# An attention-plus-MLP kernel: MLP units of one chunk and four feature blocks, paired score bursts, two uncast loads, and a new order of all work

## The chip, the cores and the metric

One core of one Trainium2 chip. The metric is the device time of one execution in microseconds (us), lower is better. A profile of one execution goes with each kernel; its span is about 1.8 us shorter than the time of the same execution. In the profiles PE is TensorE, PEld its weight loads, DVE VectorE, ACT ScalarE and POOL GpSimd. A run is called slow in the record when it is over 1.5% above the fastest of the same kernel, else fast. The clock is the share of its full rate that TensorE was granted; at half rate its matmuls start twice as far apart.

## The reference

Four batches, eight heads, 768 tokens, head size 64: causal attention with a decay per head and a running state, then an MLP with ELU on 3072 tokens of width 512.

```python
for b in range(nb):                                   # along the sequence
    intra = (qb @ kb.T * Dmask) @ vb                   # inside the block
    inter = (qb * lam_pow) @ kv_state                  # from the blocks before
    out[:, :, sl] = intra + inter
    kv_state = lam_block * kv_state + (kb * rev_pow).T @ vb
x = attn_out.transpose(0, 2, 1, 3).reshape(3072, 512)
h = x @ w_in                                           # 512 x 2048
g = where(h > 0, h, exp(min(h, 0)) - 1)
return g @ w_out                                       # 2048 x 512
```

## The kernel before

The work is cut into 24 chunks of 128 tokens (chunk g is batch g mod 4, step g div 4). For each chunk TensorE transposes q and k (later chunks: by DMA), computes the scores S, multiplies them with v and with the state (P), and updates the state (U). The MLP takes three chunks at a time, one block of 128 features per slot. In the profiles psT, psS, psO and psU hold the results of transposes, scores, attention output and state update, psH and psM those of the MLP's first and second product; wi and wo are its weights, g is the ELU's output. The code is shortened, its comments are mine:

```python
TC = 3; MT = TC * L                       # 3 chunks, 384 columns
WI = [2, 2, 4, 4, 4]; WO = [4, 4, 4, 4]   # blocks per weight transfer
M2_FIRST = 12                             # first slot with a second product
POOL_ORDER = "i0 i1 l3 k0 i2 k1 i3 k2 i4 l4 k3 o0 k4 k5 o1 l6 o2 k6 k7 o3 l8 l10"

def mm1(s):                               # one feature block of 3 chunks
    m, n = divmod(s, NFT)
    pH = ps.tile([128, MT], FP32, tag=tag, ...)
    for kk in range(NHP):                 # 4 matmuls of 384 columns
        nc.tensor.matmul(pH[:], lhsT=wi16[i][:, kk, j*128:(j+1)*128],
                         rhs=xt[m][:, kk, :], start=(kk == 0), stop=(kk == NHP - 1))
    e = msb.tile([128, MT], FP32, tag="e", bufs=3, ...)
    nc.scalar.activation(e[:], pH[:], AF.Exp)
    nc.scalar.activation(pH[:], pH[:], AF.Relu)
    return e, pH
...
def regular(g, f):                        # attention of chunk g from slot f
    at(f, lambda: att_S(g))               # 8 matmuls on 64 rows, then 2 masks
    at(f + 2, lambda: att_PI(g, (0, 1)))
    at(f + 2, lambda: att_PI(g, (2, 3)))
    at(f + 3, lambda: att_X(g))
    at(f + 3, lambda: att_U(g))
...
emit_load(0, "q")                         # GpSimd (software) queue, cast fp32 -> fp16
emit_load(0, "k")
...
att_T_pe(0, ...); att_S(0); att_T_pe(1, ...); att_S(1); open_PV_X(0, ...)
att_T_pe(2, ...); att_S(2); open_PV_X(1, ...); open_PV_X(2, ...)
# only then the first mm1
```

## Time and profile before

| | before |
|---|---|
| time, median of the runs beside the result | 231.94 us (231.19 to 233.45) |
| span of the profiled execution (timed 233.71) | 231.9 us |
| first score, first unit of product 1, first of product 2 | 7.61, 17.09, 39.73 us |
| full stretch, one chunk | 24.94 us for three = 8.31 us |
| from the last matmul's end (227.9) to the end | 4.0 us |

This is TensorE's timeline of the kernel before, with start, length, line, operation and count:

```profile
39.73 1.46 PE L364 MATMUL psM<-wo,g 128*128 128x512 f16 x3
40.99 1.49 PE L339 MATMUL psH<-xt,wi 128*128 128x384 f16 x4
42.27 0.92 PE L364 MATMUL psM<-wo,g 128*128 128x512 f16 x3
43.02 0.81 PE L339 MATMUL psH<-xt,wi 128*128 128x384 f16 x4
```

Starts are 1.26 and 1.28 us apart where 0.65 is the full pace. After the 2.15 us wait that ends at 39.19 the array runs at half rate for about 3 us.

### The profile page before, as it was taken

The numbers are of one execution on the slowest core, as the hardware profiler recorded it, in microseconds if no ns is written. First come the engines' busy times: TensorE is split into PE (matmuls) and PEld (weight loads), VectorE is DVE, ScalarE is ACT, GpSimd is POOL, SyncE is SP. The second block draws the span as 40 slices with busy tenths as digits, with TensorE's granted clock in tenths as the row PEclk, the third lists the DMA queues.
The fourth block names the chain that finished last, engine by engine and source line by source line (L and its number), as shares of the span: only waits on it lengthen the run. The fifth ranks groups of instructions, "written<-read, shape, count | busy, mean of one in ns | idle before, by whom it ended". The sixth has DMA issues, their size and how long they took to land.

```text
span 231.9 us, 4127 instructions
## 1 busy us (share of the span) xinstructions
PE 208.7 (90%) x1504; PEld 117.7 (51%) x1504; DVE 144.7 (62%) x274; ACT 134.0 (58%) x306; POOL 87.5 (38%) x101
## 2 busy tenths in 40 slices
PE   1488666989999999999999999999999999999993
PEld 0364443546546555555654555555555555555441
DVE  6665867476686676766667667676765657344410
ACT  4437765366575565755566555755576557667610
POOL 8999274797773274445256242200000000000000
PEclk9999998899999999999999999999999999999998
DMA  7999999999999998997977990540033001100312
GB/s 50 137 160 195 177 149 164 156 148 156 156 132 211 165 132 34 184 156 117 93 47 189 147 74 3 173 98 3 1 115 68 3 0 71 69 0 0 136 48 90
DMA packets 100324, 24.39 MB, mean 105 GB/s; under 512 B 92496, under 2 KB 97360, under 8 KB 100304
## 3 DMA queue, kind: packets, MB, share of 16 engines
q0 software_dynamic: 79152, 13.63, 81.6%
q1 hardware_dynamic: 21152, 10.50, 21.9%
q8 instruction: 12, 0.20, 0.4%
q14 instruction: 8, 0.07, 0.1%
HBM read 27.27 MB, written 6.29 MB: 145 GB/s over the span
## 4 chain that ended last, share of the span: by engine, by line
PE 76%; POOL 8%; DVE 6%; DMA 4%; ACT 3%; issue 2%; POOLq 0%; ACTq 0%; DVEq 0%
PE psM L364 34%; PE psH L339 31%; DMA kn<-in_k_dram 4%; PE psO L278 4%; PE psS L257 3%; POOL qn L93 2%; PE psO L283 2%; POOL wi L118 2%; POOL kn L93 2%; POOL vz L97 2%; DVE st L321 1%; POOL kd L205 1%; PE psU L305 1%; DVE g L350 1%; DVE qT L230 1%
## 5 line engine op out<-in xcount | busy, mean ns | idle before, releaser
L339 PE MATMUL psH<-xt,wi 128*128 128x384 f16 x512 | 104.5, 329 | 3.3 <-DVE g L350 1.4
L350 DVE SCALAR_TENSOR_TENSOR g<-e,psH 128x384 f16<-128x384 f32 x128 | 70.4, 552 | 58.9 <-ACT psH L345 58.1
L344 ACT ACTIVATE e<-psH 128x384 f32<-128x384 f32 x128 | 63.0, 492 | 72.5 <-PE psH L339 72.0
L364 PE MATMUL psM<-wo,g 128*128 128x512 f16 x384 | 101.6, 382 | 0.0
L339 PEld LDWEIGHTS <-wi 128*128 128x128 f16 x512 | 50.0, 99 | 49.3 <-issue 6.3
L345 ACT ACTIVATE psH<-psH 128x384 f32<-128x384 f32 x128 | 62.4, 487 | 0.0
L364 PEld LDWEIGHTS <-g 128*128 128x128 f16 x384 | 34.8, 98 | 29.5 <-issue 1.0
L263 DVE TENSOR_TENSOR pp<-psS,mask 128x512 f16<-128x512 f32 x48 | 30.9, 686 | 5.7 <-PE psS L257 4.0
L205 POOL TENSOR_TENSOR kd<-kn,ks 128x512 f16<-128x512 f16 x20 | 20.9, 1048 | 11.2 <-DMA kn<-in_k_dram 10.3
L317 POOL TENSOR_TENSOR stt<-st,upp 64x256 f32<-64x256 f16 x24 | 14.6, 607 | 27.3 <-DVE st L321 26.4
L97 POOL DMA_DIRECT2D vz<-in_v_dram x14 | 15.3, 1095 | 21.0 <-PE psU L305 17.6
L257 PE MATMUL psS<-qT,kT 64*128 64x128 f16 x192 | 10.4, 232 | 7.6 <-DVE st L321 2.1
L278 PE MATMUL psO<-pp,vz 128*128 128x128 f16 x168 | 16.2, 219 | 0.0
L93 POOL DMA_DIRECT2D qn<-in_q_dram x14 | 15.8, 1128 | 0.8 <-POOLq L509 0.8
L93 POOL DMA_DIRECT2D kn<-in_k_dram x14 | 15.2, 1089 | 1.0 <-DMA qn<-in_q_dram 1.0
L321 DVE TENSOR_TENSOR st<-stt,psU 64x256 f16<-64x256 f32 x32 | 13.3, 417 | 3.3 <-PE psU L305 1.0
L278 PEld LDWEIGHTS <-vz 128*128 128x128 f16 x168 | 13.6, 98 | 2.6
L283 PE MATMUL psO<-qT,st 128*128 128x128 f16 x80 | 14.4, 219 | 0.0
L257 PEld LDWEIGHTS <-kT 64*128 64x128 f16 x192 | 6.1, 99 | 15.0 <-issue 6.1
L379 ACT COPY osb<-psM 128x512 f32<-128x512 f32 (+1 forms) x16 | 8.5, 576 | 8.7 <-PE psM L364 8.7
L377 DVE COPY osb<-psM 128x512 f32<-128x512 f32 (+1 forms) x9 | 5.9, 656 | 8.4 <-PE psM L364 5.7
L296 DVE TENSOR_TENSOR xt<-psO,qs 128x512 f16<-128x512 f32 x16 | 10.9, 683 | 0.0
(48 smaller groups left out, 83.7 us busy)
## 6 DMA issues: line engine op xcount, KB each, us to landing
out_dram<-osb SPq DMA_DIRECT2D x23, 256.0 KB, 2.3
qn<-in_q_dram POOLq DMA_DIRECT2D x10, 256.0 KB, 9.1
kn<-in_k_dram POOLq DMA_DIRECT2D x10, 256.0 KB, 9.8
vz<-in_v_dram POOLq DMA_DIRECT2D x10, 256.0 KB, 9.5
wo<-in_moe_w_out_dram POOLq DMA_DIRECT2D x4, 512.0 KB, 9.0
wi<-in_moe_w_in_dram POOLq DMA_DIRECT2D x3, 512.0 KB, 7.9
qn<-in_q_dram POOLq DMA_DIRECT2D x4, 128.0 KB, 4.1
kn<-in_k_dram POOLq DMA_DIRECT2D x4, 128.0 KB, 4.3
```

Source lines behind the costliest of these rows:

```text
L93: nc.gpsimd.dma_start(out=t[:].rearrange("p b h d -> p (b h) d"), in_=src(x))
L97: nc.gpsimd.dma_start(out=t[:, :, 0::2, :].rearrange("p b h d -> p (b h) d"), in_=src(v))
L205: nc.gpsimd.tensor_tensor(out=kd[:], in0=of(kg, g), in1=ks[:].unsqueeze(2).broadcast_to([128, H, 64]), op=ALU.mult,)
L257: nc.tensor.matmul(pts[hh][:, hp, :], lhsT=kt[r, hp, :], rhs=qt[r, hp, :], start=True, stop=True,)
L263: nc.vector.tensor_tensor(out=P[:], in0=pts[hh][:], in1=mask[:, hh::2, :], op=ALU.mult)
L278: nc.tensor.matmul(po[:, hp, :], lhsT=vt[:, b0 : b0 + 2, :], rhs=Pt[(g, hh)][:, hp, :], start=(hh == 0), stop=(hh == 1 and cb == 0), skip_ ...
L283: nc.tensor.matmul(po[:, hp, :], lhsT=st[b][cb % 2][:, hp, :], rhs=qt[:, hp, :], start=False, stop=True, skip_group_check=True,)
L339: nc.tensor.matmul(pH[:], lhsT=wi16[i][:, kk, j * 128 : (j + 1) * 128], rhs=xt[m][:, kk, :], start=(kk == 0), stop=(kk == NHP - 1),)
L344: nc.scalar.activation(e[:], pH[:], AF.Exp)
L345: nc.scalar.activation(pH[:], pH[:], AF.Relu)
L350: nc.vector.scalar_tensor_tensor(out=g[:], in0=e[:], scalar=-1.0, in1=r[:], op0=ALU.add, op1=ALU.min)
L364: nc.tensor.matmul(psM[m][c][:], lhsT=gts[s][:, c * 128 : (c + 1) * 128], rhs=wo16[i][:, j, :], start=(n == 0), stop=(n == NFT - 1),)
```

## The change

The intent: begin the MLP as soon as one chunk is ready, give TensorE in each moment something whose data has come, and switch less often to the 64-row matmuls of the scores. Both weight matrices come in pieces of two blocks, the two interleaved. The whole order is a written list: `1:g:j` is product 1 of chunk g and blocks 4j to 4j+3, `2:g:j` product 2; T, S, E, P, U are transposes, scores, their masks, output and state update; V, Z, v, z zero buffers. The core of the diff, shortened, with comments of mine:

```diff
-    TC = 3
-    M2_FIRST = 12
-    WI = [2, 2, 4, 4, 4]
-    WO = [4, 4, 4, 4]
-    POOL_ORDER = "i0 i1 l3 k0 i2 k1 i3 k2 i4 l4 k3 o0 ... l10"
+    FB = 4
+    GPE = 10                     # transposes on TensorE for 10 chunks, was 8
+    WI = [2] * 8
+    WO = [2] * 8
+    POOL_ORDER = ("iota q1 k1 v1 v0 i1 i0 k2 q2 v2 o0 o1 i3 i2 q3 i5 k3 o2 d0 o3 ... v10")
+    RAW = "q0 k0"                # uncast, on the hardware queue
+    FIRST = "q0:0 c0 k0:1 c1 c2"
+    OPEN = (
+        "V0 Z1 z1 V1 z0 v3:1 Z0 z3 z2 T0 T1 S0 S1 P0 P1 1:0:0 T2 1:1:0 S2 2:0:0 Z2 P2 1:2:0 "
+        "1:0:1 2:1:0 1:1:1 U0 T3 2:2:0 1:2:1 S3 2:0:1 2:1:1 1:0:2 1:1:2 P3 2:2:1 ... S8:9 2:6:0 E9")
...
-            nc.tensor.matmul(
-                pH[:], lhsT=wi16[i][:, kk, j * 128 : (j + 1) * 128],
-                rhs=xt[m][:, kk, :], start=(kk == 0), stop=(kk == NHP - 1),
-            )
+        for f in range(FB):
+            i, w = wi_of[j * FB + f]
+            for kk in range(NHP):
+                nc.tensor.matmul(
+                    pH[:, f, :], lhsT=wi16[i][:, kk, w * 128 : (w + 1) * 128],
+                    rhs=xt[g][:, kk, :], start=(kk == 0), stop=(kk == NHP - 1),
+                )
...
+            else:                # "S4:5": both score bursts, then the mask of the first
+                att_S(a[0])
+                att_S(a[1])
+                att_E(a[0])
...
+    prog[-1] += ":1"             # the last product 2 is computed in two column halves
```

## The prediction

> **What bounds the kernel now.** I read the page's busy rows first, then the groups, then TensorE's timeline in the opening, in the middle and at the end.
>
> ```profile
> span 231.9 us, 4127 instructions
> PE 208.7 (90%) x1504; PEld 117.7 (51%) x1504; DVE 144.7 (62%) x274; ACT 134.0 (58%) x306; POOL 87.5 (38%) x101
> PE   1488666989999999999999999999999999999993
> PEclk9999998899999999999999999999999999999998
> GB/s 50 137 160 195 177 149 164 156 148 156 156 132 211 165 132 34 184 156 117 93 47 189 147 74 3 173 98 3 1 115 68 3 0 71 69 0 0 136 48 90
> L339 PE MATMUL psH<-xt,wi 128*128 128x384 f16 x512 | 104.5, 329 | 3.3 <-DVE g L350 1.4
> L364 PE MATMUL psM<-wo,g 128*128 128x512 f16 x384 | 101.6, 382 | 0.0
> L263 DVE TENSOR_TENSOR pp<-psS,mask 128x512 f16<-128x512 f32 x48 | 30.9, 686 | 5.7 <-PE psS L257 4.0
> ```
>
> TensorE is full from about slice 9 (5.8 us each) to the end and half empty before; nothing else is over 62%. The means of 329 and 382 ns are latencies; the pace has to be read from starts. TensorE's timeline, in the opening and in the full stretch:
>
> ```profile
> 17.09 3.48 PE L339 MATMUL psH<-xt,wi 128*128 128x384 f16 x16
> 22.06 0.82 PE L339 MATMUL psH<-xt,wi 128*128 128x384 f16 x4 [1.05 <-DMA wi<-in_moe_w_in_dram]
> 30.50 0.40 PE L223 MATMUL psT<-ident,kn 128*128 128x128 f16 x4 [1.28 <-DMA kn<-in_k_dram]
> 39.19 0.61 PE L257 MATMUL psS<-qT,kT 64*128 64x128 f16 x8 [2.15 <-DVE st L321]
> ...
> 115.25 0.81 PE L364 MATMUL psM<-wo,g 128*128 128x512 f16 x3
> 115.90 0.81 PE L339 MATMUL psH<-xt,wi 128*128 128x384 f16 x4
> 116.64 0.40 PE L257 MATMUL psS<-qT,kT 64*128 64x128 f16 x8
> 116.97 0.82 PE L364 MATMUL psM<-wo,g 128*128 128x512 f16 x3
> 117.63 0.81 PE L339 MATMUL psH<-xt,wi 128*128 128x384 f16 x4
> ```
>
> Start to start, four 384-column matmuls take 0.65 us (162.5 ns each), three of 512 columns 0.65 us (215.5 ns), and eight score matmuls 0.33 us plus about 0.10 us lost around them (the preceding four start 0.74 before instead of 0.65). Elsewhere in that timeline twelve 128-column matmuls, each with its own weight load, run from 43.67 to 44.34: 56 ns each.
>
> At those paces TensorE's work is 512 x 0.1625 = 83.2 (first MLP product), 384 x 0.2155 = 82.8 (second), attention output 272 x 0.056 = 15.2, state updates 80 x 0.056 = 4.5, transposes of 8 chunks 64 x 0.056 = 3.6, scores 24 x 0.43 = 10.3: 199.6 us. The span is 32.3 more. Up to 17.09 only 3.9 us of that work (24 transposes, 3 scores, 24 output products) is done: 13.2 lost. From 17.09 to 40 the counts (52 of the 384-column kind, 20 updates, 20 outputs, 24 transposes, 3 scores) make 13.3 of 22.9: 9.6 lost. The tail after the last matmul (227.9) is 4.0. That leaves 5.5 for everything from 40 to 218, most of it before 70. So the gain to be had lies in the first 40 us, where the MLP waits until three chunks have gone through attention, and then for weights, keys and states.
>
> **What the Trainium skill says.** "TensorE: Matmul & The Clock Gate", section "Wait — 56ns, not 53.3ns?", gives N ÷ 2.4 GHz + about 2.5 ns start to start: 55.6 ns at 128 columns, 215.7 at 512. The trace agrees (56; 162.5 at 384; 215.5). Hence cutting 384 columns into 3 x 128 costs about 3 x 56 - 162.5 = 5.5 ns per old matmul. The same page, "What's actually happening", says that an idle array falls to half rate. The trace agrees: at 8.15 four transposes take 0.54 us, and in slices 7 and 8, after the idle ends at 39.19, the clock row shows 8. "DMA: Bandwidth & Descriptors", section "Issuing engines are not separate DMA queues", says that all issuers share 16 engines and that a second issuer saves only issue time. So the two loads moved to the hardware queue free about 1.9 us of GpSimd issue (1.06 + 0.88 in the trace), not bandwidth. "VectorE: DVE Perf Modes", section "The TRN2 errata — SBUF-src ops pay a fixed extra latency per instruction", says what each operation pays besides its elements; here VectorE's ELU takes 552 ns at 384 columns, and the score product 686 at 512, so I estimate 690 for the new 512-column ELU.
>
> **The change part by part.**
>
> *MLP units.* A unit is now 16 matmuls of 128 columns (0.90 us) or 4 of 512 (0.86). 1536 x 0.056 = 86.0, so +2.8 us. ELU, Exp and Relu go from 128 to 96 each: VectorE 96 x 0.69 = 66 instead of 70; ScalarE's pair at about 0.62 each (copies of 512 columns take 0.59) 119 instead of 125. Per chunk of 8.3 us of TensorE, ScalarE has about 5.6 and VectorE 5.6: no new bound in the steady part.
>
> *Scores in pairs.* 24 bursts become 14 (four single, ten double): 24 x 0.33 + 14 x 0.10 = 9.3, so -1.0 us. Transposes by TensorE for ten chunks instead of eight: 80 x 0.056 = 4.5, +0.9. New sum of TensorE's work: 202.3, that is +2.7.
>
> *The opening.* The arrival of data is the ruler. In slices 2 to 8 the transfers move 163 GB/s on average, and with the first load landed at 4.8 us this puts the old fourth key pair (4.19 MB of half-precision data in the order of issue) at 4.8 + 4.06/0.163 = 29.7; TensorE waited for it until 30.5. In the new order, counting the uncast k as 0.2 MB: weights i0, i1 at 12.5, o1 at 18, i2 at 21, k3 24.5, o3 28, i7 38, k4 43. VectorE and ScalarE reach the first scores at about 9.7 (five zeroings of 0.4 to 0.6 us stand on ScalarE before the first kT copy; in the old kernel scores start at 7.6), the first output is copied by 13.4, and the first MLP unit starts at 13.5 instead of 17.09. It goes on with whatever chunk is ready, and the second product no longer waits until 39.7 but starts when o1 lands, near 18-19. From 21 on the listed order has nearly always something whose data has come; each pair of units waits for an ELU about 2.1 us after the end of the unit two before. Walking the order with these durations I get to 47 at the end of unit 1:3:2 (first product, chunk 3, third group of four blocks; 2:... is the second product). Up to there TensorE does 16 x 0.90 + 12 x 0.86 + 6 x 0.45 (transposes) + 4 x 0.43 + 4 x 0.45 + 2 x 0.22 = 31.3 us, so 15.7 are lost. The old kernel loses 13.2 + 9.6 + about 2 = 24.8 by then. Gain: 9 us.
>
> *48 to 75 us.* Four transposed chunks, five pairs of score products, six updates of which four take four VectorE operations, and eleven ELUs: VectorE has about 25.7 us of work beside 29 of TensorE. That is tight, and I put 3 us of waiting on it (the old kernel loses about 3.5 after 47 in all).
>
> *Rest.* 1 us of small ELU waits in the steady part. Tail: the last output goes out in two halves, so one 0.37 us copy and then the store, 3.1 us in the trace: 3.5 instead of 4.0.
>
> Sum: 202.3 + 15.7 + 3.0 + 1.0 + 3.5 = 225.5. The timed median of before is within 0.4 of its profiled span, so I take the span for the time.
>
> **The rivals.**
>
> *Weight loads bind.* 128-column matmuls need a load every 56 ns, 16 in a row and up to 30 with neighbours; the trace shows only runs of 12 at that pace. Were a pair to take 64 ns, 1536 x 8 ns = 12 us would eat the gain: about 237. Against it: those 12 run at full pace, and a 0.86 us unit of four loads follows nearly every burst, so the queue can refill. I give it 5%.
>
> *The opening stays as long.* If the many short rows of q, k, v or the uncast loads slow the transfers to the 137 of slice 2, k4 lands at 49 and the gain shrinks to 4 us: about 230. For it: the new order asks for all weights before q4, k4; the old one had k4 at 30.5. Against it: chunks 0 to 3 alone hold 28 us of MLP work, which covers that.
>
> *VectorE in the middle.* With 25.7 of 29 us taken, each score product ahead of an ELU holds up the two psH buffers; if that costs 6 us instead of 3: 228.5.
>
> *Better than I walk.* TensorE unbroken from 21 us on, with the waits in the middle filled by the order: 220.
>
> **Range and chances.** The gain of the opening (9, give or take 4) against 2.7 of added work decides it; the error of the walk is about 4 us either way, hence 220.5 to 230. The 2% line is 227.6, 2.1 above the middle, so faster 0.68, within 2% 0.30; slower needs the weight-load rival or a deadlock of orders: 0.02.
>
> **What would show it.** Right: first psH matmul near 13.5 us; first psM near 18-19; 16 psH matmuls in about 0.90 us start to start; one chunk per 8.3 us in the steady part; transposes of chunk 4 near 45; ScalarE and VectorE under 70%; a tail of 3.5. Wrong: psH units of 1.0 us or more with issue as the reason; psH waiting for g throughout; chunk 4's keys after 48; first scores far from 9.7; a clock row under 9 after 25 us.

## The result, and the profile after

The changed kernel takes 223.12 us (222.66 to 223.24, 4 runs) against 231.94 beside it: ratio 0.9608, 95% interval 0.9556 to 0.966. Ratios here are the mean time of one kernel's fast runs over that of the other's of the same rounds, so not quite the ratio of the medians quoted. The point forecast was 225.5, the range 220.5 to 230.

Rows of the page of the changed kernel (busy times; busy tenths, clock and transfer rate in 40 slices of 5.5 us; groups):

```profile
span 221.4 us, 6086 instructions
PE 207.1 (94%) x2548; PEld 156.3 (71%) x2548; DVE 138.6 (63%) x238; ACT 134.8 (61%) x255; POOL 88.6 (40%) x102
PE   0598999999999999999999999999999999999993
PEclk9999999999999999999999999999999999999999
GB/s 114 169 182 186 195 200 167 139 169 120 166 140 181 127 164 135 141 84 93 143 100 100 132 108 95 144 0 98 94 3 98 96 3 47 52 1 50 47 3 95
L388 PE MATMUL psH<-xt,wi 128*128 128x128 f16 x1536 | 102.2, 220 | 1.8 <-ACT xt L333 0.7
L409 PE MATMUL psM<-wo,g 128*128 128x512 f16 (+1 forms) x388 | 97.6, 377 | 0.8 <-DVE osb L422 0.5
```

TensorE is at 80% or more from the third slice instead of about the eighth, its clock row never falls under 9, and the first slice moves 114 GB/s instead of 50. Neither row tells the whole opening: the first unit's 16 matmuls take 1.71 us (13.36 to 15.07 below), half the later pace, though slice 3 shows a 9 for the clock.

TensorE's timeline of the changed kernel, opening, full stretch and end:

```profile
9.48 1.09 PE L300 MATMUL psS<-qT,kT 64*128 64x128 f16 x16 [1.26 <-ACT kT L289]
...
13.36 1.91 PE L388 MATMUL psH<-xt,wi 128*128 128x128 f16 x16
15.07 0.63 PE L281 MATMUL psT<-ident,qn 128*128 128x128 f16 x4
...
17.43 1.04 PE L409 MATMUL psM<-wo,g 128*128 128x512 f16 x4
...
28.71 1.95 PE L388 MATMUL psH<-xt,wi 128*128 128x128 f16 x32
30.50 0.61 PE L322 MATMUL psO<-pp,vz 128*128 128x128 f16 x8
...
45.00 1.06 PE L388 MATMUL psH<-xt,wi 128*128 128x128 f16 x16
45.99 0.62 PE L300 MATMUL psS<-qT,kT 64*128 64x128 f16 x16
...
85.86 1.07 PE L388 MATMUL psH<-xt,wi 128*128 128x128 f16 x16 [0.45 <-DVE g L376]
86.86 0.62 PE L300 MATMUL psS<-qT,kT 64*128 64x128 f16 x16
87.41 1.04 PE L409 MATMUL psM<-wo,g 128*128 128x512 f16 x4
88.29 1.06 PE L388 MATMUL psH<-xt,wi 128*128 128x128 f16 x16
...
217.73 0.60 PE L409 MATMUL psM<-wo,g 128*128 128x256 f16 x4 [0.52 <-DVE osb L422]
```

The 32 matmuls from 28.71 to 30.50 take 56 ns each with a weight load apiece: the weight loads do not bind in such a run. The score bursts repeat every 16.50 us (86.86, 103.36, 119.86), so a chunk costs 8.25 us. By stretches (length; busy time and count of TensorE, weight loads, VectorE, ScalarE, GpSimd; clock; transfers), the changed kernel does not wait from 100 to 133 us, and it idles 0.23 us in the stretch in which VectorE is nearly full:

```profile
50.00:60.00 10.00, 9.77 (x135) 8.03 (x134) 9.45 (x17) 7.10 (x14) 10.00 (x10) 1.00 1.56 141
100.00:133.00 33.00, 33.00 (x418) 25.04 (x417) 21.51 (x36) 19.45 (x37) 15.76 (x18) 1.00 1.10 113
```

Where the 10.5 us between the two profiled spans come from, at the paces of the traces (a lone score burst at 0.445 us, a pair at 0.67; see a1_single_scores for these): TensorE's work goes from 199.9 to 201.4, the tail from 4.0 to 3.6 (3.1 after the last matmul and the 0.52 us wait), and what is left, waiting and half rate, from 28.0 to 16.4. The gain is 11.6 us less of these. The profiled execution of before was one of its slower ones (233.71 timed), which is the reason that this difference is larger than the 8.8 us of the medians.

### The profile page after: what moved, and what is told of

It is laid out like the page before. It is cut to its first block, busy times and chain, and to the rows that moved or that the text cites. A ratio compares the mean times of both kernels' runs of the same rounds, so it can differ in the third digit from the quotient of the medians.

```text
span 221.4 us, 6086 instructions
## 1 busy us (share of the span) xinstructions
PE 207.1 (94%) x2548; PEld 156.3 (71%) x2548; DVE 138.6 (63%) x238; ACT 134.8 (61%) x255; POOL 88.6 (40%) x102
## 4 chain that ended last, share of the span: by engine, by line
PE 79%; DVE 11%; ACT 5%; DMA 2%; issue 1%; SPq 0%; DVEq 0%; ACTq 0%
PE psH L388 34%; PE psM L409 33%; PE psO L322 5%; DVE g L376 3%; PE psS L300 3%; DVE stt L356 2%; DMA raw_k<-in_k_dram 2%; PE psO L327 2%; DVE pp L309 2%; PE psU L344 2%; DVE qT L288 1%; DVE st L360 1%; ACT e L393 1%; ACT psH L394 1%; PE psT L281 1%
## 5 line engine op out<-in xcount | busy, mean ns | idle before, releaser
L388 PEld LDWEIGHTS <-wi 128*128 128x128 f16 x1536 | 94.0, 98 | 22.0 <-issue 2.2
L388 PE MATMUL psH<-xt,wi 128*128 128x128 f16 x1536 | 102.2, 220 | 1.8 <-ACT xt L333 0.7
L393 ACT ACTIVATE e<-psH 128x512 f32<-128x512 f32 x96 | 57.3, 597 | 68.3 <-PE psH L388 68.0
L409 PE MATMUL psM<-wo,g 128*128 128x512 f16 (+1 forms) x388 | 97.6, 377 | 0.8 <-DVE osb L422 0.5
L376 DVE SCALAR_TENSOR_TENSOR g<-e,psH 128x512 f16<-128x512 f32 x96 | 65.6, 684 | 44.1 <-ACT psH L394 42.8
L394 ACT ACTIVATE psH<-psH 128x512 f32<-128x512 f32 x96 | 56.9, 593 | 0.0
L335 DVE TENSOR_TENSOR xt<-psO,qs 128x512 f16<-128x512 f32 x14 | 9.7, 691 | 11.9 <-PE psO L327 11.9
L424 ACT COPY osb<-psM 128x512 f32<-128x512 f32 (+1 forms) x24 | 13.9, 579 | 4.5 <-PE psM L409 4.5
L288 DVE TENSOR_TENSOR qT<-psT,qs 128x512 f16<-128x512 f16 x10 | 6.6, 681 | 5.2 <-PE psT L281 5.2
L281 PE MATMUL psT<-ident,qn 128*128 128x128 f16 x40 | 4.6, 247 | 5.4 <-DVE qn L122 5.4
L333 ACT CAST xt<-psO 128x512 f16<-128x512 f32 x10 | 5.9, 588 | 6.0 <-PE psO L322 4.0
```

Of the source, the lines that this page charges most:

```text
L376: nc.vector.scalar_tensor_tensor(out=g[:], in0=e[:], scalar=-1.0, in1=r[:], op0=ALU.add, op1=ALU.min)
L388: nc.tensor.matmul(pH[:, f, :], lhsT=wi16[i][:, kk, w * 128 : (w + 1) * 128], rhs=xt[g][:, kk, :], start=(kk == 0), stop=(kk == NHP - 1),)
L409: nc.tensor.matmul(psM[g][:, cols], lhsT=gts[(g, j)][:, f, :], rhs=wo16[i][:, w, cols], start=first and f == 0, stop=end and f == FB - 1, ...
```

## The experiments

Names with a start from the changed kernel, with b from the kernel before. Each ran with five timed rounds and a profile. They came in three groups, each on one chip with its own runs of the kernel before (medians 233.65, 234.19 and 233.39, with a scatter from 231.5 to 237.2). Since the changed kernel scatters by under 1 us and the kernel before by several, I compare the a-kernels by their own times and spans and quote the ratios only beside them. The changed kernel itself ran beside the result and in the third group only, so the differences quoted for a1 to a6 cross groups; "over the first measurement" is meant where nothing else is said. All results were correct.

| run | time, us (range) | ratio to before | profiled span |
|---|---|---|---|
| a0_again (unchanged) | 222.56 (222.43 to 223.37) | 0.957 | 220.7 |
| a1_single_scores | 225.65 (225.06 to 226.21) | 0.967 | 224.0 |
| a2_soft_q0k0 | 224.22 (223.79 to 224.62) | 0.961 | 222.0 |
| a3_three_first | 226.57 (226.24 to 228.46) | 0.973 | 225.0 |
| a4_wi_first | 234.98 (234.45 to 235.4) | 1.007 | 232.7 |
| a5_zeros_late | 222.11 (221.96 to 223.04) | 0.953 | 220.4 |
| a6_tail_banks | 222.39 (221.61 to 222.96) | 0.953 | 220.4 |
| a7_both | 221.64 (221.43 to 222.67) | 0.952 | 220.8 |
| a8_three_undone | 231.38 (230.41 to 231.84) | 0.993 | 229.8 |
| b1_split128 | 233.29 (232.86 to 233.8) | 1.000 | 232.0 |
| b2_raw_q0k0 | 230.20 (230.12 to 230.69) | 0.987 | 228.4 |
| b3_kept_warm | 232.35 (231.33 to 232.85) | 0.997 | 230.4 |

**a0_again.** The changed kernel itself, no edit, in the third group.

> The changed kernel itself, as the yardstick on this chip for the three that run beside it: 223 to 224.5 us, profiled span near 221.4.

222.56 us, half a microsecond under the first measurement. Spans of 220.7 to 221.6 over its six executions. So differences of about half a microsecond between groups are not read below.

**a1_single_scores.** Scores in bursts of one chunk.

```diff
-            (f"S{g}:{g + 1}", AT["S"]), (f"E{g + 1}", AT["S"] + 1),
+            (f"S{g}", AT["S"]), (f"S{g + 1}", AT["S"] + 1),
```

(and likewise S4, S6, S8 in the opening list.)

> The changed kernel with the scores of each chunk in a burst of its own, one unit apart (24 bursts instead of 14). My theory: each burst costs about 0.11 us of exposed weight load beside its 0.33, so +1.1 us over the changed kernel: about 224.2, ratio to before near 0.966. Rival, that the pairing is a main source of the gain: 226 or more. Rival, that the pairing is worth nothing because TensorE waits elsewhere anyway: 223.1.

225.65 us, 2.5 over the first measurement of the changed kernel and 2.6 in span: more than twice the 1.1 expected. TensorE's timeline of this run:

```profile
89.17 1.06 PE L388 MATMUL psH<-xt,wi 128*128 128x128 f16 x16
90.16 0.40 PE L300 MATMUL psS<-qT,kT 64*128 64x128 f16 x8
90.49 1.04 PE L409 MATMUL psM<-wo,g 128*128 128x512 f16 x4
91.37 1.06 PE L388 MATMUL psH<-xt,wi 128*128 128x128 f16 x16
```

Eight scores stand for 0.33 us (90.16 to 90.49), sixteen in the changed kernel for 0.55 (86.86 to 87.41). So eight cost 0.22 and each burst a fixed 0.11 on top; with the 0.10 before it and 0.02 after it, a burst costs about 0.22 beside its work. Ten fewer bursts are 2.2 us (the scores of chunks 0 and 1 stand together in both kernels, 16 at 9.48); the period of two chunks confirms it (16.71 us here, from 87.97 to 104.68, against 16.50). I had taken the 0.33 as pure work. The runs show the size of this cost and not its cause.

**a2_soft_q0k0.** The two loads back on the software queue.

```diff
-    RAW = "q0 k0"
-    FIRST = "q0:0 c0 k0:1 c1 c2"
-        "iota q1 k1 v1 v0 ...
+    RAW = ""
+    FIRST = "c0 c1 c2"
+        "iota q0 k0 q1 k1 v1 v0 ...
```

> The changed kernel with q, k of chunk 0 cast by the software queue again, first in its order; no cast instructions. My theory: the hardware queue saves only about 1.9 us of GpSimd issue for all that follows, and the first scores wait for zeroings on ScalarE in any case: 223.1 to 224.6 (the first MLP unit at 13.4 to 14.5 us). Rival, that the two uncast loads carry the early start: 226 or more, first MLP unit after 15.5 us.

224.22 us, +1.1 (span +0.6). The first unit starts at 13.82 instead of 13.36. The second unit still runs at half pace (1.85 us to the next start, 16.35 to 18.20, instead of 1.19), and the scores of chunk 4 start at 47.09 instead of 45.99. As expected, and the rival falls; but the ratio (0.961) is that of the change itself, so the 1.1 us rest on comparing groups and on the trace.

**a3_three_first.** No MLP unit before the third chunk.

```diff
-        ... P0 P1 1:0:0 T2 1:1:0 S2 2:0:0 Z2 P2 1:2:0 "
+        ... P0 P1 T2 S2 Z2 P2 1:0:0 1:1:0 2:0:0 1:2:0 "
```

> The changed kernel with the old rule of starting: no MLP unit before the third chunk has gone through attention (two first-product units and one second-product unit move behind the output of chunk 2, nothing else moves). My theory, that the early start fills TensorE's idle time: +2 to +3 us, 225 to 226. Rival, that data arrival sets the end of the opening and the early units are hidden anyway: 223.1 to 223.6.

226.57 us, +3.4 (span +3.6), somewhat over the expected 2 to 3: the first unit starts at 17.98, the first of product 2 at 21.79, and no later slack takes the delay up (chunk 4's scores start at 49.16 instead of 45.99). The rival, that arrival of data hides the early units, falls. Not all of it is waiting:

```profile
17.98 3.62 PE L388 MATMUL psH<-xt,wi 128*128 128x128 f16 x32
21.79 1.64 PE L409 MATMUL psM<-wo,g 128*128 128x512 f16 x4 [0.19 <-DVE g L376]
23.27 1.95 PE L388 MATMUL psH<-xt,wi 128*128 128x128 f16 x32
```

The 32 matmuls take about 3.5 us instead of 1.8, the four of 512 columns 1.48 instead of 0.86: 2.3 us over full pace, where the changed kernel's first two units lose 1.0. So I estimate that about 1.3 of the 3.4 us are half pace.

**a4_wi_first.** All of the first weight matrix before the second.

```diff
-        ... q2 v2 o0 o1 i3 i2 q3 i5 k3 o2 d0 o3 i4 v3 o5 o4 d2 o7 i6 d3 d1 i7 o6 q4
+        ... q2 v2 i3 i2 q3 i5 k3 i4 d0 i6 i7 v3 o0 o1 d2 o2 o3 d3 d1 o5 o4 o7 o6 q4
```

> The changed kernel with all eight pieces of the first weight matrix issued before any of the second, as the kernel before has it; TensorE's order is not touched. My theory, that the interleaved arrival of the two matrices is what lets both products start early: TensorE stands at the first second-product unit (17.4 us in the changed kernel) until the piece lands near 24, 4 to 7 us lost: 227 to 230. Rival, that arrival is not binding: under 224.

234.98 us: 11.9 slower, as slow as the kernel before (ratio 1.007), and more than the 4 to 7 expected. TensorE's timeline:

```profile
27.23 1.01 PE L409 MATMUL psM<-wo,g 128*128 128x512 f16 x2 [9.94 <-DMA wo<-in_moe_w_out_dram]
28.51 1.01 PE L409 MATMUL psM<-wo,g 128*128 128x512 f16 x2 [0.27 <-DMA wo<-in_moe_w_out_dram]
```

TensorE keeps its written order and stands 9.94 us for the first piece of the second matrix; the long idle also costs clock (0.978 on average, 0.999 in the changed kernel). The order of arrival and the order of work are one thing: this list without the matching transfers wins nothing. It does not say that weights-first with a work order of its own would lose as much.

**a8_three_undone.** The edits of a1, a2 and a3 together.

> The changed kernel with three parts undone together: single score bursts, q and k of chunk 0 on the software queue, no MLP unit before the third chunk. Alone they moved the profiled span by +2.6, +0.6 and +3.6. If they are independent: +6.8, span near 228.2, about 2 us under the kernel before; that rest is then the interleaved arrival of both weight matrices and the order of units. If the early start already holds what the queue gives: +6.2.

231.38 us, 8.8 over a0_again, span +9.1. The sum of +6.8 was taken against the first measurement's span of 221.4, against which a8 is +8.4; against a0_again's 220.7 the three alone make +8.9. So the spans do not settle whether they are more than additive. The traces show that they depend on each other in the opening: with all three gone TensorE's wait for q transfers grows (8.1 us in three waits, 5.1 in two with the loads alone moved back), by 2.97 us for q of chunk 2 that neither a2 nor a3 waits for. What is left of the change (interleaved weights, one-chunk units, ten chunks transposed by TensorE, the halved last product) is then worth about 0.7% against the kernel before; no run takes this remainder apart.

**b1_split128.** Only the narrow matmuls, in the kernel before.

```diff
-        for kk in range(NHP):
-            nc.tensor.matmul(pH[:], lhsT=..., rhs=xt[m][:, kk, :], ...)
+        for c in range(TC):
+            cc = slice(c * L, (c + 1) * L)
+            for kk in range(NHP):
+                nc.tensor.matmul(pH[:, cc], lhsT=..., rhs=xt[m][:, kk, cc], ...)
```

> The kernel before with each 384-column matmul of the first product cut into three of 128, each with its own weight load; nothing else. My theory: 12 x 56 ns in place of 4 x 162.5 ns for 128 units is +2.8 us, ratio 1.012, with some of it hidden in the opening. Rival, weight loads every 56 ns can't be kept up (64 ns a pair): +12 us, ratio 1.05. Rival, cutting is free: 1.000.

Ratio 1.000 (0.995 to 1.0045). The time says free, the trace says not: TensorE's timeline of this run has

```profile
98.20 0.81 PE L366 MATMUL psM<-wo,g 128*128 128x512 f16 x3
98.85 0.83 PE L341 MATMUL psH<-xt,wi 128*128 128x128 f16 x12
...
100.61 0.83 PE L341 MATMUL psH<-xt,wi 128*128 128x128 f16 x12
101.28 0.81 PE L366 MATMUL psM<-wo,g 128*128 128x512 f16 x3
```

0.67 us for twelve instead of 0.65 for four, which is 56 ns each and 128 x 0.02 = 2.6 us in all, near the 2.8 of the prediction. In exchange the wait at 39.75 is 1.71 us instead of 2.15 and no half rate follows: from 0.56 us behind at this point (39.75 against 39.19) the run is 0.95 ahead at the next output matmuls (42.72 against 43.67). It has its half rate earlier, from 25.1 to about 28.6 after waits of 2.32 and 1.06 us. The two nearly cancel; that the kernel before loses time to the clock was my reading, so I tested it there (b3_kept_warm). The rival of 64 ns a pair falls.

**b2_raw_q0k0.** Only the two uncast loads, in the kernel before.

```diff
-    emit_load(0, "q")
-    emit_load(0, "k")
+    for wn, x, tiles in (("q", q, qg), ("k", k, kg)):
+        raw[wn] = asb.tile([128, H, 64], FP32, ...)
+        nc.sync.dma_start(out=raw[wn][:], in_=x[0, :, 0:L].rearrange("h p d -> p h d"))
...
+    nc.vector.tensor_copy(qg[0][:, 0], raw["q"][:])
     emit_qs()
+    nc.scalar.copy(kg[0][:, 0], raw["k"][:])
```

> The kernel before with only q, k of chunk 0 loaded uncast on the hardware queue and cast on VectorE and ScalarE. My theory: a part of the change that brings little alone, since the same 16 engines move more bytes and three chunks of attention still stand before the MLP: -1.0 to +0.5 us, ratio 0.996 to 1.002. Rival, that it carries a good part of the gain: 0.985 or less.

230.20 us, ratio 0.987 (0.983 to 0.991): a miss, the part alone brings more than I allowed. The first scores are later than before (7.98 against 7.61), but GpSimd issues everything else about 1.9 us sooner, the transfer rate of the first slice is 112 GB/s instead of 50, k of chunk 4 is there when TensorE comes to it at 29.16 (before: waited until 30.50), and the wait that brings half rate is 1.73 us and brings none. Against the four quickest runs of the kernel before in its group (231.76 to 232.59) it gains 1.6 to 2.4 us, about the issue time saved; that the rest of the ratio is the half rate of the others is my reading, not shown.

**b3_kept_warm.** Needless matmuls in the idle stretch of the kernel before.

```diff
+    def warm():
+        psM[0] = [ps.tile([128, DM], FP32, tag=f"psM{i}", ...) for i in range(TC)]
+        for _ in range(8):
+            nc.tensor.matmul(psM[0][0][:], lhsT=wi16[0][:, 0, 0:128],
+                             rhs=wi16[2][:, 0, :], start=True, stop=True)
     def regular(g, f):
+        if g == 5:
+            at(f, warm)
```

> The kernel before with eight needless 512-column matmuls (about 1.7 us, into a bank that is overwritten afterwards) ahead of the scores that wait 2.15 us at 39.19. The kernel before scatters from 231.7 to 236.6 us, and in its trace the matmuls after this wait run at half pace (three of 512 columns in 1.26 us, not 0.65). Theory, that the idle stretch makes the array fall to half rate in a part of the runs and that this is the scatter: all runs near 231.5 to 232.5, ratio 0.993, no half pace at 39 to 43. Rival, that the scatter has another source: the same scatter as the kernel before beside it.

All six runs lie from 231.33 to 232.85; of the nine fast runs of the kernel before beside them five lie from 233.0 to 234.1. TensorE's timeline:

```profile
37.51 1.89 PE L408 MATMUL psM<-wi,wi 128*128 128x512 f16 x8
39.82 0.40 PE L257 MATMUL psS<-qT,kT 64*128 64x128 f16 x8 [0.42 <-DVE st L321]
40.15 0.82 PE L364 MATMUL psM<-wo,g 128*128 128x512 f16 x3
40.81 0.81 PE L339 MATMUL psH<-xt,wi 128*128 128x384 f16 x4
```

With the stretch filled, the next matmuls run at full pace (0.66 us for three). So the idle stretch is the source of the half rate in the profiled execution, and, as the narrower spread says, of most of the scatter. Some lower clock is left: four of the six runs show 0.991 or 0.992, and their traces were not kept. By ratio (0.997, 0.992 to 1.0015) the mean gain is not clear of noise; two runs of the kernel before (237.2) count as slow and are left out.

**a5_zeros_late, a6_tail_banks, a7_both.** Two improvements, alone and together.

```diff
-        "V0 Z1 z1 V1 z0 v3:1 Z0 z3 z2 T0 T1 S0 S1 P0 P1 ...        # a5
+        "T0 T1 S0 S1 V0 Z1 z1 V1 z0 v3:1 Z0 z3 z2 P0 P1 ...
-        halves = [slice(0, DM // 2), slice(DM // 2, DM)] if last else [slice(0, DM)]   # a6
+        halves = [slice(0, DM // 2), slice(DM // 2, DM)] if n == 2 else [slice(0, DM)]
+        # n = 2 for the last chunk: psM[g] is two tiles of 256 columns, in banks M0 and A
```

> The changed kernel with the nine zeroings of the opening moved behind the scores of chunks 0 and 1. In the trace of the changed kernel five of them hold ScalarE until 8.87 us while the transposed k of chunk 0 has been ready for copying since about 7.3, and no TensorE wait on a transfer shows. My theory: scores start near 8.1 instead of 9.5, the first MLP unit near 12, and the end comes 0.5 to 1.3 us sooner: about 222.2. Rival, that weight arrival takes its place at once: 223.1.

> The changed kernel with the last chunk's output kept in two PSUM banks, one for each half, so that the last four matmuls need not wait for VectorE's copy of the first half (0.52 us in the trace). My theory: -0.5 us, 222.6. Rival, that the store of the first half ends last anyway: no change.

> The changed kernel with both improvements together (zeroings behind the first scores, last chunk in two PSUM banks). Each took 1.0 us off the profiled span alone, at opposite ends of the program. Theory, that they add: 2.0 us off, span near 219.4, about 1.9 us under the yardstick. Rival, that the earlier opening is given back: only 1.0 off.

a5 takes 222.11 us and a6 222.39; in their traces the first scores start at 8.17 and the first MLP unit at 12.05 (a5), and the 0.52 us wait at the end is gone (a6). Neither is clear of a0_again's range. Together they take 221.64 against 222.56 in the same group: 0.9 us, not the 1.9 expected. The 1.9 came from single spans of a5 and a6 (220.4) against 221.4 in another group; against a0_again's 220.7 each saves only 0.3, so the shortfall is first of all one of the yardstick. In the profiled run of a7, which is its slowest (222.67), TensorE now waits 0.8 us for a piece of the first weight matrix, and chunk 4's scores start at 46.20, no sooner than in a0_again (45.86): the earlier opening was given back to weight arrival in that run, as the rival had it. In the five other runs the span is 219.7 to 220.0 (a0_again: 220.7 to 221.6), so part of it stays. By medians a7_both is 0.4% quicker than the changed kernel; five of its six runs lie below all of a0_again's.

## Why the prediction was right

The mechanism held: most of the gain is idle time of TensorE in the first 46 us, got by starting with one chunk and by weights that arrive in the order of use (a3, a4), and it is reduced by the narrower matmuls (b1's trace). The forecast of 225.5 stood 2.4 us over the time, and this closeness is partly luck: the sum is one of spans, and the measured span is 221.4, 4.1 us lower. I took the span for the time because the timed median of before was near its profiled span, but that profile was of a slower execution (233.71 us timed); the changed kernel's span is 1.7 us under its own time. Step by step:

- *MLP units:* 0.90 and 0.86 us as predicted once the array is at full pace (the first unit took 1.71); 128-column matmuls at 56 ns in runs of 32. The rival on weight loads had no share.
- *Scores in pairs:* a mis-sized term. Predicted -1.0, measured -2.2 (a1), all of it after the opening. A burst has 0.22 us beside its work, not 0.10, which could have been seen only from bursts of two lengths.
- *Opening:* predicted first scores 9.7, first unit 13.5, second product 18 to 19, end of unit 1:3:2 at 47 with 15.7 us lost. Measured 9.48, 13.36, 17.43, 45.9 and 14.6. Transfers ran at 169 to 200 GB/s from the second slice to the sixth rather than the 163 I had carried over.
- *48 to 75 us:* predicted 3 us of waiting on VectorE. From 45.9 to 85.8 TensorE's listed work is 38.6 of 39.9 us, so about 1.3 were lost, though VectorE was busy 9.45 of 10 us in one stretch. That a full engine off the path had enough lead is my reading; I made no run on it.
- *Rest and tail:* predicted 1.0 and 3.5; measured none between 100 and 199 us (about 0.5 remain elsewhere), and 3.6. The two halves of the last output save less than they could: the last four matmuls wait 0.52 us for the copy of the first half (a6 removes it).
- *What the prediction undervalued:* the half rate. I named the slices at clock 8 but gave the change nothing for avoiding them. b3 points to the idle stretch behind them for most of the old kernel's scatter; the changed kernel waits at most 0.67 us at once after 10 us, and its runs agree within 0.6 us (0.9 in a0_again).

## What to carry to other kernels

When one engine is full for most of the program, look at its opening as a schedule of arrivals: small units that need one input each, and transfers cut and ordered as the units use them, fill it, and both orders must be changed together. Count what a burst costs beside its work from bursts of two lengths before you judge merging. Treat a stretch of two idle microseconds of TensorE as more than its length, since half rate can follow it: here a wait of 2.15 us was followed by matmuls that took 1.5 us more than at full pace, and it went with the scatter.

## What the Trainium skill lacked or had wrong

- "TensorE: Matmul & The Clock Gate", section "Why this matters for your kernels", warns of idle gaps over about 3 us. Here a wait of 2.15 us, after a stretch of patchy work, was followed by about 3 us at half rate; waits of 1.71 to 1.73 us at the same place (b1, b2) were not, though b1 has half rate after waits of 2.32 and 1.06 us earlier.
- No page gives a figure for switching between 128-row matmuls and a burst of 64-row ones ("TensorEngine Tiling (Array Packing)", section "Key Properties", says that changing the tiling mode drains TensorE, and no more). The runs show about 0.22 us per burst (16.71 against 16.50 us per pair of chunks).
- "DMA: Bandwidth & Descriptors", section "Issuing engines are not separate DMA queues", calls the issue time saved by a second issuer usually small. That it saves only issue time agrees with the traces, but at the start of a program, when the engines stand idle, it was worth 1.6 to 2.4 us of 232 alone (b2) (50 against 112 GB/s in the first slice).
